# Last layer of a fused attention and MoE kernel: low parts one product later, weight work moved to other slots

## Chip, cores and metric

The kernel runs on one core of a Trainium2 chip. The metric is the device time of one execution in microseconds (us). A core has five engines that run beside each other, each with a queue of its own that it works through in order: TensorE (PE, with its weight loads as PEld), VectorE (DVE), ScalarE (ACT), GpSimd (POOL) and SyncE (SP, which here issues DMAs).

## What is computed

Attention with a window of 128 keys and four sink keys for every query, then a layer with eight experts, then a layer that multiplies two products elementwise:

```python
x = attention(q, k, v)                     # 1536 tokens x 512
P = sinkhorn(exp(x @ w_gate))              # 8 rounds, 1536 x 8
for e in range(8):                         # w1[e] 512 x 1024, w2[e] 1024 x 512
    out += P[:, e:e+1] * (np.maximum(x @ w1[e], 0) @ w2[e])
x = out
return ((x @ w_a) * (x @ w_b)) @ w_out     # w_a, w_b 512 x 1536, w_out 1536 x 512
```

All values are float32. The chip's fast matmul type drops bits, so a value is kept as a high part (a rounded copy) and a low part (value minus high part), and a product takes three matmuls: high x high, high x low, low x high (`mm3`, line 90).

## The kernel before

After the attention part, the two layers run as a row of steps. Tokens come in two batches of 768. The expert layer has 64 steps (`STEPS`): steps 0 to 31 are batch 0, 32 to 63 are batch 1. Each step takes one block of 256 hidden columns of one expert. The first matrix product of a step is done with a seven-product scheme (Strassen-like sums of blocks of x and of the weights): `product(s, j)` for j = 0 to 6, each six matmuls of 384 columns into a PSUM bank (128x384 in the profile). `leave(s, j, give)` takes the result out of the bank: j = 0 is an ACT copy (L353), 2 is the DVE sum at L357, 3 is L359, 4 the pair L369 and L370 (L364 and L365 in most steps of the expert layer), 5 is L373, 6 is L377 (L361 there). The last layer uses banks 6 and 7 in turn, so a product waits for the sum that empties its bank: product 4 for L357, product 5 for L359, product 0 of the next step for L373.

The last layer has twelve rounds q (`STEPS2`, six for each batch). A round is two steps, numbered on from 64: part 0 (x by `w_a`) and part 1 (x by `w_b`). In part 0, `keep` copies four results to `av[f][t]` (ACT, L567; f is the block of hidden columns, t the half of the batch). In part 1, `multiply` (L569 to L573) multiplies the kept value by the new one (DVE, L571), copies the high part to `hid` (ACT, L572) and hands the low part (`lower`, DVE, L169) to a list. It does so at product 1 for (f, t) = (0, 0), at product 4 for (1, 1), at product 5 for (0, 1); (1, 0) belongs to product 6 and is given one product later, in the next part 0.

Two lists set the order by hand. What is in `later` is issued at the end of the same product (`flush`), and what is in `late` moves to `later` then, so it is issued at the end of the product after it. The names `av` have tiles of their own: `first_p`, `room`, `room`, `extra`.

The second matrix product of round q - 1 runs in round q, six blocks of 128 tokens (`second2`, six matmuls of 512 columns each; 128x512 in the profile). In part 0 it does tokens 3, 4, 5 (half t = 1), in part 1 tokens 0, 1, 2. Its first block comes right after product 0 of part 0, and the third matmul of that block is the first that reads the low part (0, 1) of the round before. In rounds 1 to 4 (`turning`), batch 1 of x is transposed on TensorE beside this, and the blocks come after products 0, 1 and 5; in the other rounds after 0, 2 and 5.

Weights are prepared beside the matmuls. `pair_parts` makes one step's seven weight blocks: sums on POOL (L188, L191, L196, L204), high parts on ACT (L189, L193, L201, L208, L212, L218), low parts on DVE and, for the rows of the second product, on POOL (all L169: `ring<-raw` for loaded blocks, `ring<-room` for sums). `double_parts` packs a block of the last layer's weights to 29 bits a value and writes it back to memory (ACT L232, DVE L234, L235, L239, L243). A call of `work()` goes on with both by a bit. `quiet` (line 122) lists the expert steps at whose place in the queue of items one block is packed; there are 36. In the last layer `work()` is called once after every product, but not after product 0 of part 0 while x is turned.

In steps 31 and 32 the sums of x for the next batch are split too (`renew`, `flat<-xt` in the profile), on DVE for their low parts.

Of the kernel before, what the change touches and what calls it, by code (L numbers as in the profile page):

```python
# [33 lines left out]
PAIRS = NF // 2  # L34
# [12 lines left out]
def fused_kernel(  # L47
# [16 lines left out]
    pe, act, dve, pool, sp = nc.tensor, nc.scalar, nc.vector, nc.gpsimd, nc.sync  # L64
# [38 lines left out]
    STEPS, STEPS2 = B * E * PAIRS, B * PAIRS2  # L103
# [15 lines left out]

    quiet = [s for s in range(4, STEPS - 2) if s % PAIRS != 2 and abs(s - STEPS // 2 - 2) > 1]
    made = 0
    for s in range(STEPS):
        e, i = divmod(s % (E * PAIRS), PAIRS)
# [17 lines left out]
    def place(s):  # L143
        return s - 2 * (s >= STEPS + 2 * PAIRS2)
    loaded, taken, started, pairs = [0], [0], [0], [0]
    going, gone, ready, held = [], set(), set(), [False]
    later, late, whole = [], [], []
# [20 lines left out]
    def lower(src, hi, lo, eng):  # L168
        eng.tensor_tensor(out=lo, in0=src, in1=hi.bitcast(F32), op=ALU.subtract)  # L169
# [111 lines left out]
    def x_sums(x, space):  # L281

        t1, t2, t3, t4 = (space[:, n * S:(n + 1) * S].rearrange("p (k t) -> p k t", k=2) for n in range(4))
        b11, b12, b21, b22 = (x[:, 2 * i:2 * i + 2, j * HT:(j + 1) * HT] for i in range(2) for j in range(2))
        todo = [(t1, b12, b11), (t2, b22, t1), (t3, b22, b12), (t4, t2, b21)]
        return todo, [b11, b21, t2, t3, t1, b22, t4]
# [40 lines left out]
    def product(s, j):  # L327
        made_so_far[0] += 1
        ps = target(s, j)
        w = cell(CELLS * place(s) + ORDER[j])  # L330
        for kk in range(2):
            c0, c1 = slice(kk * 128, kk * 128 + 128), slice(256 + kk * 128, 384 + kk * 128)
            t0 = slice(kk * HT, kk * HT + HT)
            mm3(
                ps, w[:, c0], w[:, c1], x_part(j, 0)[:, t0], x_part(j, 1)[:, t0],
                kk == 0 and j != 1, kk == 1, check=j > 1,
            )
# [9 lines left out]
    def leave(s, j, give):  # L347

        ps = target(s, j)
        m = mid[:, s % 2 * 3:s % 2 * 3 + 3]  # L350
        m0 = m[:, 0] if s else first_p
        if j == 0:
            act.copy(out=m0, in_=ps)  # L353
        elif j == 1:
            give(s, ps, 0, 0)
        elif j == 2:
            dve.tensor_tensor(out=m0, in0=m0, in1=ps, op=ALU.add)  # L357
        elif j == 3:
            dve.tensor_tensor(out=m[:, 1], in0=m0, in1=ps, op=ALU.add)  # L359
        elif s in LONG and j == 6:  # L360
            dve.tensor_tensor(out=m[:, 2], in0=m[:, 1], in1=ps, op=ALU.subtract)  # L361
            give(s, m[:, 2], 1, 0)
        elif s in LONG and j == 4:
            dve.tensor_tensor(out=m[:, 1], in0=m[:, 1], in1=ps, op=ALU.add)  # L364
            dve.tensor_tensor(out=m0, in0=m0, in1=ps, op=ALU.add)  # L365
            give(s, m[:, 1], 1, 1)
            give(s, m0, 0, 1)
        elif j == 4:
            dve.tensor_tensor(out=m[:, 2], in0=m[:, 1], in1=ps, op=ALU.add)  # L369
            dve.tensor_tensor(out=m0, in0=m0, in1=ps, op=ALU.add)  # L370
            give(s, m[:, 2], 1, 1)
        elif j == 5:
            dve.tensor_tensor(out=m0, in0=m0, in1=ps, op=ALU.add)  # L373
            if s not in LONG:
                give(s, m0, 0, 1)
        else:
            dve.tensor_tensor(out=m[:, 1], in0=m[:, 1], in1=ps, op=ALU.subtract)  # L377
            late.append(lambda: give(s, m[:, 1], 1, 0))

    def flush():  # L380
        todo, later[:], late[:] = list(later), list(late), []
        for f in todo:
            f()
# [65 lines left out]
    def rest():  # L449
# [32 lines left out]
        def x2_turn(c, n, home):  # L482

            kk, half = divmod(n, 2)
            ps = home[:, 0:HT]
            for t in range(CB // 2):
                pe.transpose(  # L487
                    out=ps[:, t * 128:(t + 1) * 128],
                    in_=acc[c][:, half * (CB // 2) + t, kk * 128:(kk + 1) * 128], identity=ident,
                )  # L490
            act.copy(out=x2t[c][:, kk, half * HT:(half + 1) * HT], in_=ps)
# [6 lines left out]
        def halves(todo):  # L498

            return [tuple(t[:, k] for t in todo[n]) for n, k in ((0, 0), (0, 1), (2, 0), (1, 0), (3, 0), (2, 1), (1, 1), (3, 1))]  # L500
# [12 lines left out]
        def renew(plan, r, off=()):  # L513
            for n in plan[r] if r < len(plan) else ():
                later.append(x_split(ops, RANK[n // 2] if plan is EVEN else n // 2, pool if n in off else dve, slice(n % 2, n % 2 + 1)))
# [11 lines left out]
        for s in range(1, STEPS):  # L527
            long = s in LONG
            for r in range(7):
                j = RANK[r] if long else r  # L530
# [38 lines left out]
        def multiply(s, src, f, t):  # L569
            a, h, t0 = av[f][t], hid[s // 2 % 2], slice(t * HT, t * HT + HT)  # L570
            dve.tensor_tensor(out=a, in0=a, in1=src, op=ALU.mult)  # L571
            act.copy(out=h[:, 0, f, t0], in_=a)  # L572
            later.append(lambda: lower(a, h[:, 0, f, t0], h[:, 1, f, t0], dve))  # L573

        def second2(q, t, fs=(0, 1)):
            c, u = divmod(q, PAIRS2)
            h = hid[(STEPS // 2 + q) % 2]
            t0 = slice(t * 128, t * 128 + 128)
            last = u == PAIRS2 - 1 and fs != (1,)
            row = (c * CB + t) * 128  # L580
            for f in fs:
                n = CELLS * place(STEPS + 2 * q + 1) + 7 + 2 * f
                mm3(
                    bank[t], h[:, 0, f, t0], h[:, 1, f, t0], cell(n), cell(n + 1),
                    u == 0 and f == 0, last and f == fs[-1],
                )
            if not last:
                return

            end = q == STEPS2 - 1 and t == TURN[-1]  # L590
            for d in (slice(0, DM // 2), slice(DM // 2, DM)) if end else (slice(0, DM),):
                (dve.tensor_copy if d.start else act.copy)(out=acc[1][:, t, d], in_=bank[t][:, d])
                (act if d.start else sp).dma_start(out=out[row:row + 128, d], in_=acc[1][:, t, d])

        SUMS = ((3, 3), (3, 5), (4, 2), (4, 3), (4, 4), (5, 1), (5, 2), (5, 3))
        for q in range(STEPS2 + 1):
            c, u = divmod(q, PAIRS2)
            turning = 1 <= q < 5
            AT = (0, 1, 5) if turning else (0, 2, 5)
            for part in range(2):  # L600
                n = STEPS + 2 * q + part
                for j in range(7):
                    if q < STEPS2:
                        assert place(n) in ready, n
                        product(n, j)
                        leave(n, j, (keep, multiply)[part])
                    if turning and j == 1:
                        x2_turn(1, 2 * (q - 1) + part, bank[7])
                    if q == 0 and part == 0:
                        renew(FRONT, 7 + j, (12, 13))  # L610
                    if (q, part) in ((PAIRS2 - 1, 1), (PAIRS2, 0)):

                        held[0] = q == PAIRS2 and j < 5
                        renew(BACK, 7 * (q == PAIRS2) + j, (2, 3))
                    if j in AT:
                        t = TURN[3 * part + AT.index(j)]
                        if q == STEPS2 and part == 0:

                            if j == 0:
                                for x in TURN[0:3]:  # L620
                                    second2(q - 1, x, (1,))
                            second2(q - 1, t, (0,))
                        elif q:
                            second2(q - 1, t)
                        else:
                            second(STEPS - 1, t)
                    flush()
                    if (q, part, j) == (3, 0, 3):
                        todo, ops = x_sums(x2t[1], flat_0)
                        todo = halves(todo)  # L630
                    if part == 0 and (q, j) in SUMS:
                        step_sum(pool)
                    if not (turning and part == 0 and j == 0):
                        work()
                if q < STEPS2 and q != PAIRS2 - 1:
                    for m in range(7 if part else CELLS):
                        used[CELLS * place(n) + m] = True
            if q != PAIRS2:
                done = STEPS - 1 if q == 0 else place(STEPS + 2 * q - 1)
                for m in range(7, CELLS):  # L640
                    used[CELLS * done + m] = True
# [543 lines left out]
```

## Time and profile before

| | |
|---|---|
| median of 3 runs | 1391.4 us (1391.33 to 1391.56) |
| the profiled execution | 1391.5 us |
| its span, first to last instruction | 1389.7 us |
| PE busy | 1378.1 us, 99% of the span |
| DVE, ACT, POOL busy | 965.0, 578.8, 602.8 us |
| mean granted TensorE clock | 0.999 of 2.4 GHz |

The time of an execution is 1.8 us more than the span. TensorE is busy nearly always, but the ends of matmuls are modelled in this profile, so a short stop shows better as idle time of the weight loads (PEld), which run beside the matmuls. Expert step 32 begins at 587 us of the span, the last layer at 1090 us, its last matmul ends at 1384 us.

### The profile page before, as it was taken

How to read it: one execution, taken by the hardware profiler on the slowest of the kernel's cores; microseconds unless marked ns; L12 is line 12 of the kernel's file. 1: busy time of each engine (PE TensorE's matmuls, PEld its weight loads, DVE VectorE, ACT ScalarE, POOL GpSimd, SP SyncE). 2: the span in 40 equal slices, each digit the busy share in tenths (PEclk: the TensorE clock that was granted, in tenths of full speed). 3: DMA queues.
4: the chain of work that ended last, by engine and by line, in shares of the span. 5: the costliest groups of instructions: out<-in, count | busy, mean ns of one | idle time of the engine just before them, and what ended most of it. 6: DMA issues, size and time to landing. Idle time of an engine off the chain costs nothing.

```text
span 1389.7 us, 20344 instructions
## 1 busy us (share of the span) xinstructions
PE 1378.1 (99%) x7202; PEld 1222.8 (88%) x7202; DVE 965.0 (69%) x1886; ACT 578.8 (42%) x1322; POOL 602.8 (43%) x666
## 2 busy tenths in 40 slices
PE   9999999999999999999999999999999999999998
PEld 6678989898999999898899898989899898988997
DVE  7877776777686767865666777774656866777673
ACT  8873443433333333444333333333333544444442
POOL 7884343444434343343443434343433534523430
PEclk9999999999999999999999999999999999999999
DMA  7412332334333433323342333322222122213111
GB/s 228 127 47 84 114 106 92 106 100 123 100 111 94 119 106 92 106 69 99 97 123 85 110 106 103 114 89 74 66 68 69 54 69 61 77 38 99 61 32 48
DMA packets 144811, 127.37 MB, mean 92 GB/s; under 512 B 7844, under 2 KB 116004, under 8 KB 144700
## 3 DMA queue, kind: packets, MB, share of 16 engines
q1 hardware_dynamic: 144122, 125.46, 29.8%
q8 instruction: 58, 0.95, 0.3%
q10 hardware_dynamic: 578, 0.52, 0.1%
q14 instruction: 53, 0.43, 0.1%
HBM read 112.75 MB, written 12.58 MB: 90 GB/s over the span
## 4 chain that ended last, share of the span: by engine, by line
PE 94%; DVE 2%; ACT 1%; issue 1%; POOL 1%; DMA 0%; SPq 0%; DVEq 0%; ACTq 0%; POOLq 0%
PE bank L90 89%; PE bank L918 1%; PE bank L841 1%; PE bank L899 1%; PE bank L900 1%; POOL a L874 0%; PE bank L487 0%; DVE ring L169 0%; DVE hid L169 0%; ACT ex L858 0%; ACT hid L572 0%; PE bank L308 0%; PE bank L927 0%; DMA xt<-in_v 0%; DVE mid L373 0%
## 5 line engine op out<-in xcount | busy, mean ns | idle before, releaser
L90 PE MATMUL bank<-flat,ring 128*128 128x384 f32 x3696 | 688.5, 337 | 2.8 <-DVE mid L357 1.7
L90 PEld LDWEIGHTS bank<-flat,ring 128*128 128x128 f32 x3696 | 648.7, 188 | 28.8 <-DVE mid L357 4.2
L90 PE MATMUL bank<-ring,hid 128*128 128x512 f32 x2736 | 667.4, 393 | 0.4 <-DVE hid L169 0.4
L90 PEld LDWEIGHTS bank<-ring,hid 128*128 128x128 f32 x2736 | 508.1, 188 | 100.3 <-DVE hid L169 3.5
L169 POOL TENSOR_TENSOR ring<-raw,ring 128x512 fp32r<-128x512 f32 x150 | 211.1, 1426 | 399.3 <-ACT ring L201 390.7
L341 ACT ACTIVATE hid<-mid 128x384 fp32r<-128x384 f32 x191 | 97.0, 526 | 406.7 <-DVE mid L361 273.8
L188 POOL TENSOR_TENSOR room<-raw 128x256 f32<-128x256 f32 x86 | 88.5, 1029 | 298.6 <-DVE ring L169 109.0
L361 DVE TENSOR_TENSOR mid<-mid,bank 128x384 f32<-128x384 f32 x56 | 31.0, 554 | 132.4 <-PE bank L90 132.4
L169 DVE TENSOR_TENSOR ring<-raw,ring 128x512 fp32r<-128x512 f32 (+1 forms) x172 | 118.4, 689 | 0.0
L357 DVE TENSOR_TENSOR mid<-mid,bank 128x384 f32<-128x384 f32 x87 | 47.8, 550 | 98.9 <-PE bank L90 98.9
L169 DVE TENSOR_TENSOR ring<-room,ring 128x512 fp32r<-128x512 f32 x172 | 113.1, 692 | 2.8 <-ACT ring L212 2.8
L342 DVE SCALAR_TENSOR_TENSOR hid<-mid,hid 128x384 fp32r<-128x384 f32 x191 | 102.7, 562 | 13.0 <-ACT hid L341 4.9
L341 ACT ACTIVATE hid<-bank 128x384 fp32r<-128x384 f32 x64 | 31.5, 492 | 188.9 <-PE bank L90 188.7
L191 POOL TENSOR_TENSOR room<-raw 128x256 f32<-128x256 f32 x86 | 86.1, 1001 | 8.9 <-DVE ring L169 7.2
L204 POOL TENSOR_TENSOR room<-raw,room 128x256 f32<-128x256 f32 x86 | 71.6, 833 | 6.3
L373 DVE TENSOR_TENSOR mid<-mid,bank 128x384 f32<-128x384 f32 x87 | 48.0, 551 | 30.6 <-PE bank L90 30.5
L196 POOL TENSOR_TENSOR room<-room,raw 128x256 f32<-128x256 f32 x86 | 67.2, 782 | 0.0
L359 DVE TENSOR_TENSOR mid<-mid,bank 128x384 f32<-128x384 f32 x87 | 47.5, 545 | 11.0 <-PE bank L90 11.0
L218 ACT CAST ring<-room 128x512 fp32r<-128x512 f32 x86 | 52.9, 615 | 2.0 <-POOL room L204 1.7
L212 ACT CAST ring<-room 128x512 fp32r<-128x512 f32 x86 | 53.3, 620 | 0.9 <-POOL room L196 0.9
L239 DVE SCALAR_TENSOR_TENSOR room<-raw,room 128x512 int32<-128x512 int32 x36 | 52.8, 1468 | 1.1
L189 ACT CAST ring<-raw 128x512 fp32r<-128x512 f32 x86 | 53.5, 622 | 0.0
(150 smaller groups left out, 1152.7 us busy)
## 6 DMA issues: line engine op xcount, KB each, us to landing
raw<-in_moe_w SPq DMA_DIRECT2D x256, 256.0 KB, 2.6
raw<-kept SPq DMA_DIRECT2D x66, 256.0 KB, 3.1
kept<-room SPq DMA_DIRECT2D x36, 256.0 KB, 4.4
raw<-in_moe_w_a SPq DMA_DIRECT2D x12, 512.0 KB, 4.3
raw<-in_moe_w_b SPq DMA_DIRECT2D x12, 512.0 KB, 4.0
raw<-in_moe_w_out SPq DMA_DIRECT2D x12, 512.0 KB, 4.1
out_x<-xt SPq DMA_DIRECT2D x11, 256.0 KB, 2.0
qt<-in_q SPq DMA_DIRECT2D x6, 384.0 KB, 3.9
```

Source lines behind the costliest of these rows:

```text
L90: pe.matmul(out=dst, lhsT=a, rhs=b, start=start and n == 0, stop=stop and n == 2, skip_group_check=not check,)
L169: eng.tensor_tensor(out=lo, in0=src, in1=hi.bitcast(F32), op=ALU.subtract)
L188: pool.tensor_tensor(out=s1, in0=a21, in1=a22, op=ALU.add)
L189: act.copy(out=quads(hi, 4, 6), in_=firsts)
L191: pool.tensor_tensor(out=s3, in0=a11, in1=a21, op=ALU.subtract)
L196: pool.tensor_tensor(out=s2, in0=s1, in1=a11, op=ALU.subtract)
L204: pool.tensor_tensor(out=s4, in0=a12, in1=s2, op=ALU.subtract)
L212: act.copy(out=halves[0][0], in_=halves[0][2])
L218: act.copy(out=halves[1][0], in_=halves[1][2])
L239: dve.scalar_tensor_tensor(out=fi, in0=w[:, 0::2], scalar=29, in1=fi, op0=ALU.logical_shift_right, op1=ALU.bitwise_or)
L341: act.activation(out=h[:, 0, f, t0], in_=src, func=ACTF.Relu)
L342: later.append(lambda: dve.scalar_tensor_tensor(out=h[:, 1, f, t0], in0=src, scalar=0.0, in1=h[:, 0, f, t0].bitcast(F32), op0=ALU.max, op1 ...
```

## The change

There are three edits. `quiet` leaves out step 32 as well as 33 to 35 (34 was never in it), so the packing that stood at 32 and all those after it move on by one place in the list. `multiply` hands the low part to `late` in place of `later`, except for (1, 0) and in the last part of all. And in part 0 of the turning rounds the call of `work()` after product 2 is left out, and there are two after product 5.

```diff
-    quiet = [s for s in range(4, STEPS - 2) if s % PAIRS != 2 and abs(s - STEPS // 2 - 2) > 1]
+    quiet = [s for s in range(4, STEPS - 2) if s % PAIRS != 2 and not 0 <= s - STEPS // 2 < 4]
...
             a, h, t0 = av[f][t], hid[s // 2 % 2], slice(t * HT, t * HT + HT)
             dve.tensor_tensor(out=a, in0=a, in1=src, op=ALU.mult)
             act.copy(out=h[:, 0, f, t0], in_=a)
-            later.append(lambda: lower(a, h[:, 0, f, t0], h[:, 1, f, t0], dve))
+            soon = later if f > t or s == STEPS + 2 * STEPS2 - 1 else late
+            soon.append(lambda: lower(a, h[:, 0, f, t0], h[:, 1, f, t0], dve))
...
+        PACE = (1, 1, 1, 1, 1, 1, 1), (0, 1, 0, 1, 1, 2, 1)
...
-                    if not (turning and part == 0 and j == 0):
+                    for _ in range(PACE[turning and part == 0][j]):
                         work()
```

The order of TensorE's instructions stays as it was. Three places of DVE's queue change. In the rows below names carry numbers of buffers, which have no meaning here (`bank_69` and `bank_70` are banks 6 and 7).

First place: DVE in expert step 31, from the last low part of a weight block to the high-low split of the hidden block. Before:

```order
L169 TENSOR_TENSOR ring_1350<-raw_77,ring_1350 128x256
L234 TENSOR_SCALAR room<-room 128x512
L235 TENSOR_SCALAR room<-room 128x512
L239 SCALAR_TENSOR_TENSOR room<-raw_76,room 128x512
L357 TENSOR_TENSOR mid<-mid,bank_70 128x384
L169 TENSOR_TENSOR flat<-xt,flat 128x384
L243 SCALAR_TENSOR_TENSOR room<-raw_76,room 128x512
L342 SCALAR_TENSOR_TENSOR hid_1351<-bank_69,hid_1351 128x384
```

After:

```order
L169 TENSOR_TENSOR ring_1350<-raw_77,ring_1350 128x256
L357 TENSOR_TENSOR mid<-mid,bank_70 128x384
L169 TENSOR_TENSOR flat<-xt,flat 128x384
L342 SCALAR_TENSOR_TENSOR hid_1351<-bank_69,hid_1351 128x384
```

The four operations of one packing are gone from this step; the same four stand in step 54 now, in the same places round L357. No other step of the expert layer has another order on DVE.

Second place: DVE in part 1 of a turning round (step 67), from the sum of the part before to the sum of product 3. Before:

```order
L377 TENSOR_TENSOR mid<-mid,bank_70 128x384
L571 TENSOR_TENSOR first_p<-first_p,bank_69 128x384
L169 TENSOR_TENSOR hid_1351<-first_p,hid_1351 128x384
L169 TENSOR_TENSOR ring_75<-raw_76,ring_75 128x2x256
L357 TENSOR_TENSOR mid<-mid,bank_70 128x384
L169 TENSOR_TENSOR ring_75<-raw_76,ring_75 128x256
L359 TENSOR_TENSOR mid<-mid,bank_69 128x384
```

After:

```order
L377 TENSOR_TENSOR mid<-mid,bank_70 128x384
L571 TENSOR_TENSOR first_p<-first_p,bank_69 128x384
L169 TENSOR_TENSOR ring_75<-raw_76,ring_75 128x2x256
L357 TENSOR_TENSOR mid<-mid,bank_70 128x384
L169 TENSOR_TENSOR hid_1351<-first_p,hid_1351 128x384
L169 TENSOR_TENSOR ring_75<-raw_76,ring_75 128x256
L359 TENSOR_TENSOR mid<-mid,bank_69 128x384
```

The low part (0, 0), `hid<-first_p`, went from ahead of L357 to behind it, so that two low parts now stand between L357 and L359.

Third place: DVE from product 4 of step 67 over the end of the round into step 68. Before:

```order
L369 TENSOR_TENSOR mid<-mid,bank_70 128x384
L370 TENSOR_TENSOR mid<-mid,bank_70 128x384
L571 TENSOR_TENSOR extra<-extra,mid 128x384
L169 TENSOR_TENSOR hid_1351<-extra,hid_1351 128x384
L373 TENSOR_TENSOR mid<-mid,bank_69 128x384
L571 TENSOR_TENSOR room<-room,mid 128x384
L169 TENSOR_TENSOR hid_1351<-room,hid_1351 128x384
L169 TENSOR_TENSOR ring_75<-room,ring_75 128x2x256 x2
L377 TENSOR_TENSOR mid<-mid,bank_70 128x384
L571 TENSOR_TENSOR room<-room,mid 128x384
L169 TENSOR_TENSOR hid_1351<-room,hid_1351 128x384
L357 TENSOR_TENSOR mid<-mid,bank_70 128x384
```

After:

```order
L369 TENSOR_TENSOR mid<-mid,bank_70 128x384
L370 TENSOR_TENSOR mid<-mid,bank_70 128x384
L571 TENSOR_TENSOR extra<-extra,mid 128x384
L373 TENSOR_TENSOR mid<-mid,bank_69 128x384
L571 TENSOR_TENSOR room<-room,mid 128x384
L169 TENSOR_TENSOR hid_1351<-extra,hid_1351 128x384
L169 TENSOR_TENSOR ring_75<-room,ring_75 128x2x256 x2
L377 TENSOR_TENSOR mid<-mid,bank_70 128x384
L169 TENSOR_TENSOR hid_1351<-room,hid_1351 128x384
L571 TENSOR_TENSOR room<-room,mid 128x384
L169 TENSOR_TENSOR hid_1351<-room,hid_1351 128x384
L357 TENSOR_TENSOR mid<-mid,bank_70 128x384
```

The low part (1, 1), `hid<-extra`, moved behind the multiply of product 5, and the low part (0, 1), the first `hid<-room`, behind the two low parts of weights and L377. In part 0 of the turning rounds no low part of weights stands between L357 and L359 any more; both stand behind.

## Rows read from the trace of the kernel before

**Rows 1.** The page: span, and TensorE's busy time

```profile
span 1389.7 us, 20344 instructions
PE 1378.1 (99%) x7202; PEld 1222.8 (88%) x7202; DVE 965.0 (69%) x1886; ACT 578.8 (42%) x1322; POOL 602.8 (43%) x666
```

**Rows 2.** Waits of the weight loads, 1085 to 1385 us: total, times, longest

```profile
PEld bank L90 <- DVE hid L169: 3.5, 10, 0.9
PEld bank L90 <- DVE mid L357: 1.9, 6, 0.8
PEld bank L90 <- DVE mid L359: 1.4, 3, 0.7
PEld bank L90 <- DVE mid L373: 1.0, 2, 0.6
```

**Rows 3.** Timeline, step 31: start, duration, [idle before <-releaser]

```profile
574.62 1.51 DVE L234 TENSOR_SCALAR room<-room 128x512 f32<-128x512 f32 x1
576.16 1.40 DVE L235 TENSOR_SCALAR room<-room 128x512 int32<-128x512 int32 x1
577.60 0.69 DVE L239 SCALAR_TENSOR_TENSOR room<-raw,room 128x512 int32<-128x512 int32 x1
578.21 0.55 DVE L357 TENSOR_TENSOR mid<-mid,bank 128x384 f32<-128x384 f32 x1
578.81 0.30 PEld L90 LDWEIGHTS bank<-flat,ring 128*128 128x128 f32 x2 [1.52 <-DVE mid L357]
```

**Rows 4.** Timeline, DVE in step 46, which has a packing too

```profile
815.22 0.55 DVE L357 TENSOR_TENSOR mid<-mid,bank 128x384 f32<-128x384 f32 x1 [1.29 <-PE bank L90]
```

**Rows 5.** Timeline, steps 67 and 68: end of round 1, begin of round 2

```profile
1132.18 1.29 POOL L169 TENSOR_TENSOR ring<-raw,ring 128x512 fp32r<-128x512 f32 x1 [3.23 <-ACT ring L201]
1133.43 1.47 POOL L169 TENSOR_TENSOR ring<-raw,ring 128x512 fp32r<-128x512 f32 x1
1132.68 0.55 DVE L357 TENSOR_TENSOR mid<-mid,bank 128x384 f32<-128x384 f32 x1 [0.59 <-PE bank L90]
1133.15 0.60 DVE L169 TENSOR_TENSOR ring<-raw,ring 128x256 fp32r<-128x256 f32 x1
1133.72 0.55 DVE L359 TENSOR_TENSOR mid<-mid,bank 128x384 f32<-128x384 f32 x1
1134.76 0.55 DVE L369 TENSOR_TENSOR mid<-mid,bank 128x384 f32<-128x384 f32 x1 [0.49 <-PE bank L90]
1135.23 0.55 DVE L370 TENSOR_TENSOR mid<-mid,bank 128x384 f32<-128x384 f32 x1
1136.82 0.56 DVE L169 TENSOR_TENSOR hid<-extra,hid 128x384 fp32r<-128x384 f32 x1 [0.58 <-ACT hid L572]
1139.02 0.56 DVE L169 TENSOR_TENSOR hid<-room,hid 128x384 fp32r<-128x384 f32 x1 [0.58 <-ACT hid L572]
1139.49 1.28 DVE L169 TENSOR_TENSOR ring<-room,ring 128x512 fp32r<-128x512 f32 x2
1139.63 0.77 PEld L90 LDWEIGHTS bank<-ring,hid 128*128 128x128 f32 x4 [0.30 <-DVE hid L169]
```

**Rows 6.** Timeline, DVE and POOL in step 82

```profile
1310.10 0.74 POOL L196 TENSOR_TENSOR room<-room,raw 128x256 f32<-128x256 f32 x1
1310.92 0.94 POOL L204 TENSOR_TENSOR room<-raw,room 128x256 f32<-128x256 f32 x1
1310.13 1.13 DVE L169 TENSOR_TENSOR hid<-room,hid 128x384 fp32r<-128x384 f32 x1 [0.58 <-ACT hid L572]
1311.18 1.23 DVE L169 TENSOR_TENSOR ring<-raw,ring 128x512 fp32r<-128x512 f32 x1
```

**Rows 7.** Timeline, weight loads in parts 0 of steps 70, 74 and 78

```profile
1171.12 1.01 PEld L90 LDWEIGHTS bank<-flat,ring 128*128 128x128 f32 x6 [0.71 <-DVE mid L359]
1218.07 1.97 PEld L90 LDWEIGHTS bank<-flat,ring 128*128 128x128 f32 x11 [0.47 <-DVE mid L357]
1266.33 2.06 PEld L90 LDWEIGHTS bank<-flat,ring 128*128 128x128 f32 x12 [0.17 <-DVE mid L357]
```

## Prediction

> **What bounds the kernel.** I began with the page: TensorE is busy for 1378.1 of 1389.7 us [rows 1], so a change that leaves its instructions alone can only move its stops. The ends of matmuls are modelled, so I read the stops from the waits of the weight loads. In the last layer DVE causes nearly all: 3.5 us in ten waits for a low part of `hid`, 1.9 us for L357, 1.4 us for L359, 1.0 us for L373 [rows 2]. Outside it, one stop of 1.52 us stands in step 31 [rows 3]. These 9.3 us are all that the three edits can win. Two loads follow each other after some 0.05 us anyway, so a stop costs about 0.05 us less than its row says.
>
> Then I read the timeline at the end of a round, since all ten waits for `hid` are there, at the ends of rounds 1 to 10. The low part (0, 1) runs on DVE from 1139.02 for 0.56 us, so until 1139.58 [rows 5], and the weight load that needs it starts at 1139.63, idle before it for 0.30 us. So TensorE has no slack at this place: its position is set once a round by the end of that low part. What DVE does between TensorE's release of L369 and this end decides the round.
>
> **Step 31, the packing that moves.** L234, L235 and L239 take 1.51, 1.40 and 0.69 us ahead of L357, and TensorE waits for L357 for 1.52 us [rows 3]. Without them L357 can start when its product ends. I take a gain of 1.47 us. The four operations come back in step 54. In step 46, which has the same order of operations there, L357 still waited 1.29 us for TensorE [rows 4]: that is the cover, and I cost the move at nothing; if the cover failed as in step 31, it would cost 1.5 us. The place of the later packings and their loads moves by one item in the same pattern of steps, which I cost at nothing for the same reason.
>
> **Parts 0 of the last layer.** With no weight work between L357 and L359 in turning rounds, and with DVE earlier after the border of the round, these stops should go [rows 7]: 0.66 us in step 70, 0.42 us in step 74, and 0.12 us each in steps 78, 80, 82 and 84 (one of four equal rows stands there). That is 1.56 us. The call of `work()` that is moved past three products ends its weight block later, but the block is for a later step, and DVE waits for TensorE at L377 after it; cost nothing.
>
> **The end of a round.** Before, from the start of L369 to the end of the low part (0, 1), DVE needs 1139.58 - 1134.76 = 4.82 us, with two waits of 0.58 us for ACT's high parts [rows 5]. The change removes both waits, but puts more operations ahead of that low part: now L369, L370, multiply, L373, multiply, low part (1, 1), two low parts of weights, L377 and only then (0, 1). By the same rows, operations that depend on nothing follow after 0.47 us (L369 to L370), one that needs the result before it after 0.59 us, a low part of weights takes 0.60 us. So: three times 0.47, then 0.59 for L373, 0.47 for the multiply, 0.47 for (1, 1), 0.60 and 0.60 for the weights with 0.11 us of waiting for ACT's second sum copy, 0.47 for L377, 0.56 for the low part, and 0.09 more because POOL's next sum then runs: 5.37 us. The low part ends 0.55 us later, and with it TensorE's anchor. The ends of rounds 6 to 10 are like this (the last part keeps its order): 5 x 0.55 = +2.75 us. The bounds are +0.35 us (no wait for ACT or POOL) and +1.0 us (POOL's next sum goes first too). Round 5 has splits of x instead of weight blocks and stops there for 0.87 us already; I take no change, with bounds of -0.8 and +0.2.
>
> **The turning rounds.** In part 1 two low parts of DVE now stand between L357 and L359, while POOL makes its own two. What happens when both engines run such operations is seen in step 82 [rows 6]: a DVE low part that takes 0.56 us alone takes 1.13 us behind L196 of POOL, as if it began when L196 was through. The next POOL operation, L204, starts 0.08 us after L196 by its row, ends late, and the next DVE operation behind it takes 1.23 us where 0.69 us is usual [rows 5 and 6]. So the engines take turns. In step 67 [rows 5] POOL's first low part starts at 1132.18 for 1.29 us, its second at 1133.43; L357 starts at 1132.68. Now (0, 0) is next on DVE, at 1133.15, waits for POOL's first (free at about 1133.34) and ends at 1133.89. POOL's second then gets its turn. It ended 1.15 us after DVE's operation before (1134.90 against 1133.75), so now at 1135.04. The weight block's low part, 0.41 us alone, ends at 1135.31, and L359 runs from 1135.23 to 1135.78, where it began at 1133.72 before. L369 follows at 1135.70 in place of 1134.76, which is 0.94 us late, and the 5.37 us follow: the low part (0, 1) ends at 1141.07 instead of 1139.58, +1.49 us. In between product 5 stops for L359; that is inside this sum, since the anchor is what counts. Rounds 1 to 4 have the same rows: 4 x 1.49 = +5.96 us.
>
> *A rule beside this.* The turns are read from starts and ends of POOL's rows [rows 5 and 6]. The Trainium skill, in "Perfetto Trace Analysis", section "GPSIMD Engine Instruction", says that a GpSimd instruction's span in a profile is to be treated as unreliable. By the rows the turning rounds cost 5.96 us; by that page the order of starts would be open, and with it the first rival below.
>
> **Round 0.** Step 65 has the same operations between L357 and L359, and one more DVE sum among them. I take the same +1.49 us. Its bounds are +0.4 us (DVE goes first) and +2.7 us (the sum delays it further).
>
> **The sum.** -1.47 - 1.56 + 2.75 + 5.96 + 1.49 = +7.2 us. The durations are from the profiled execution, 1391.5 us (a span of 1389.7 and 1.8 around it), which makes 1398.7 us; the median of the runs is 0.1 us lower, so I predict 1398.6 us.
>
> **Rivals.**
>
> *DVE goes first.* If DVE's weight block gets in ahead of POOL's second low part in step 67, L359 ends at about 1134.7 and L369 is on time. Then the turning rounds cost 4 x 0.55 and round 0 some 0.9: -1.47 - 1.56 + 2.75 + 2.20 + 0.9 = +2.8, so 1394.2 us. Against it: the operation of POOL that was waiting went first [rows 6]. For it: the legend of the profile itself calls POOL's spans rough, and 0.4 us lie between the two starts in question (1133.43 and some 1133.8).
>
> *The waits go for good: faster.* If the low part (0, 1) ended before its load is due, which is 0.30 us before 1139.63 [rows 5], all the stops for DVE could go [rows 2, 3]: 9.3 us less some 20 times 0.05, 1383 us. It decides at one point: the chain from L369 must take under 4.5 us. The removal of two waits of 0.58 us speaks for it. Against it, nine operations of 0.47 to 0.60 us now stand ahead of this low part, and their busy time alone is over 4.5 us.
>
> *Little comes of it.* If the stalls at the ends of rounds turn out half as large, because weight blocks are done earlier than I think or stops merge, gains and losses cancel: 1391.4 us. That the change would not do what it says is ruled out by the order of DVE's queue; only its effect is open.
>
> **Chances and range.** A difference of over 0.2%, 2.8 us, is about what a measurement of this kernel can tell from no change. I give my forecast 0.64, DVE first 0.18 (half of it within 2.8 us, half above), little 0.09, the waits going for good 0.08, and 0.01 to more than 1401 us, where low parts lose their turn to POOL at every end of a round. So slower is 0.64 + 0.09 + 0.01 = 0.74, same 0.09 + 0.09 = 0.18, faster 0.08. The range takes in the forecast and DVE first, with their bounds: down to 1392.8 us (that rival with round 0 at +0.4 and all nine ends of rounds at +0.45) and up to 1400.8 us (the forecast with round 0 at +2.7 and rounds 6 to 10 at +0.75). The forecast alone reaches from 1396.5 us (round 0 at +0.4, rounds 6 to 10 at +0.35) to 1400.8 us.
>
> **What would show it.** In the changed profile step 31 has no stop for L357, and step 54 none. The load after the low part (0, 1) still waits for `hid`, 0.8 us in place of 0.30. In the turning parts 1 the weight loads wait about 1.4 us for L359, and DVE's weight low part ahead of it takes some 1.5 us. I am wrong if the round's end shows no wait for `hid`, or if L359 in step 67 comes within 0.5 us of L357's end.

## The result and the profile after

The changed kernel takes 1401.63 us (median of 6 runs, 1400.15 to 1403.4) where the kernel before takes 1391.37 us beside it (1391.21 to 1391.58): ratio 1.0073, interval 1.0063 to 1.0083. It is slower, as forecast, but the median lies 0.8 us above the forecast range. The profiled execution took 1400.16 us, with a span of 1398.4 us: 8.7 us more than the span before, where the sum said 7.2. Line numbers of the changed kernel are one higher from L573 on and two higher from L596 on; of the lines named here this concerns one alone, the output copy, which was L592 and is L593.

The page shows the same work as before [rows 1]:

```profile
span 1398.4 us, 20359 instructions
PE 1377.7 (99%) x7202; PEld 1224.3 (88%) x7202; DVE 964.2 (69%) x1886; ACT 580.2 (41%) x1322; POOL 607.5 (43%) x666
```

So the time went into stops. The waits of the weight loads in the last layer (total, times, longest), which answer to [rows 2]:

```profile
PEld bank L90 <- DVE hid L169: 10.4, 11, 2.3
PEld bank L90 <- DVE mid L359: 8.9, 6, 2.5
PEld bank L90 <- ACT acc L491: 1.1, 4, 0.3
PEld bank L90 <- DVE mid L373: 0.4, 1, 0.4
```

L357 is gone from the list, and the waits for L491 are as before (1.1 us in four). The waits for `hid` have tripled, those for L359 are six times as long. The stop in step 31 [rows 3] is gone too; DVE waits there for TensorE now:

```profile
576.58 0.55 DVE L357 TENSOR_TENSOR mid<-mid,bank 128x384 f32<-128x384 f32 x1 [2.48 <-PE bank L90]
```

In step 54, where the packing went, L357 keeps a margin of 1.29 us for TensorE, as the cover in [rows 4] said.

The timeline of DVE and POOL from the middle of step 67 to the load after the low part (0, 1), which answers to [rows 5]:

```profile
1132.95 2.85 POOL L169 TENSOR_TENSOR ring<-raw,ring 128x512 fp32r<-128x512 f32 x2 [2.24 <-ACT ring L201]
...
1133.45 0.55 DVE L357 TENSOR_TENSOR mid<-mid,bank 128x384 f32<-128x384 f32 x1 [1.73 <-PE bank L90]
1133.92 0.73 DVE L169 TENSOR_TENSOR hid<-first_p,hid 128x384 fp32r<-128x384 f32 x1
1134.58 1.50 DVE L169 TENSOR_TENSOR ring<-raw,ring 128x256 fp32r<-128x256 f32 x1
1136.00 0.54 DVE L359 TENSOR_TENSOR mid<-mid,bank 128x384 f32<-128x384 f32 x1
1136.65 0.55 DVE L369 TENSOR_TENSOR mid<-mid,bank 128x384 f32<-128x384 f32 x1
...
1136.60 1.00 PEld L90 LDWEIGHTS bank<-flat,ring 128*128 128x128 f32 x6 [1.42 <-DVE mid L359]
...
1141.37 0.63 DVE L169 TENSOR_TENSOR hid<-room,hid 128x384 fp32r<-128x384 f32 x1
...
1142.05 0.76 PEld L90 LDWEIGHTS bank<-ring,hid 128*128 128x128 f32 x4 [0.63 <-DVE hid L169]
```

From L357 to the end of the weight block's low part DVE needs 2.63 us here, and needed 1.07 us before. The low part (0, 1) then ends at 1142.00, 5.35 us after the start of L369; the sum said 5.37.

Round 0 is worse. In step 65 DVE and POOL do this:

```profile
1106.61 2.83 POOL L169 TENSOR_TENSOR ring<-raw,ring 128x512 fp32r<-128x512 f32 x2
...
1105.98 0.75 DVE L473 SCALAR_TENSOR_TENSOR xt<-bank,P,xt 128x512 f32<-128x512 f32 x1 [0.29 <-PE bank L90]
1106.65 1.67 DVE L169 TENSOR_TENSOR hid<-first_p,hid 128x384 fp32r<-128x384 f32 x1
1108.24 1.48 DVE L169 TENSOR_TENSOR ring<-raw,ring 128x256 fp32r<-128x256 f32 x1
1109.64 0.54 DVE L359 TENSOR_TENSOR mid<-mid,bank 128x384 f32<-128x384 f32 x1
...
1110.23 0.99 PEld L90 LDWEIGHTS bank<-flat,ring 128*128 128x128 f32 x6 [2.52 <-DVE mid L359]
```

Here POOL's first low part starts 0.04 us ahead of the low part (0, 0), which takes 1.67 us in place of 0.55, and the weight block's takes 1.48 in place of 0.42: both lose a turn. In step 67 POOL's first had started 0.97 us ahead of (0, 0) and was nearly through, so only the second of DVE's loses a turn in full.

The shift of the changed kernel against the one before, place by place, is read from the starts of the same matmuls in both traces (product 1 of a part 0 to the next; a stop of before that went is counted apart):

| place | forecast, us | measured, us |
|---|---|---|
| steps 31 and 35, stops for L357 gone | -1.47 | -1.80 |
| parts 0: steps 70, 74, and 78 to 84 | -1.56 | -1.64 |
| round 0 | +1.49 | +2.56 |
| rounds 1 to 4 | +5.96 | +6.50 |
| round 6 | +0.55 | +1.40 |
| rounds 7 to 10 | +2.20 | +1.84 |
| after the last round | 0 | -0.24 |
| sum | +7.2 | +8.6 |

Round 5, for which the forecast took no change, has no row of its own: its whole shift of -0.49 us stands in the second row. The stop of step 74 that went is most of it (0.42 us). Beside that, a stop for L359 in part 1 grew by 0.47 us and the stops at the end of the round shrank by 0.45 us, so that the forecast of no change came out by cancelling.

The table is for the profiled execution. That the median is 1.5 us above it is a second difference, and it lies in the spread of the runs. Before, 6 runs lie within 0.4 us; the changed kernel's 6 runs spread over 3.3 us, and their order is that of their mean granted clock: 0.999 in those of 1400.15 and 1400.16 us, 0.998 in those of 1401.32, 1401.94 and 1402.16 us, 0.997 in that of 1403.4 us.

### The profile page after: what moved, and what is told of

Its sections match the earlier page's. It is cut to its first block, busy times and chain, and to the rows that moved or that the text cites. A ratio compares the mean times of both kernels' runs of the same rounds, so it can differ in the third digit from the quotient of the medians.

```text
span 1398.4 us, 20359 instructions
## 1 busy us (share of the span) xinstructions
PE 1377.7 (99%) x7202; PEld 1224.3 (88%) x7202; DVE 964.2 (69%) x1886; ACT 580.2 (41%) x1322; POOL 607.5 (43%) x666
## 4 chain that ended last, share of the span: by engine, by line
PE 92%; DVE 4%; ACT 2%; issue 1%; POOL 0%; DVEq 0%; ACTq 0%
PE bank L90 86%; PE bank L920 1%; PE bank L843 1%; DVE ring L169 1%; ACT hid L572 1%; PE bank L901 1%; DVE hid L169 1%; PE bank L902 1%; DVE mid L369 0%; ACT ex L860 0%; ACT ring L218 0%; PE bank L487 0%; DVE mid L377 0%; DVE mid L370 0%; DVE extra L571 0%
## 5 line engine op out<-in xcount | busy, mean ns | idle before, releaser
L357 DVE TENSOR_TENSOR mid<-mid,bank 128x384 f32<-128x384 f32 x87 | 47.9, 550 | 112.8 <-PE bank L90 112.5
L359 DVE TENSOR_TENSOR mid<-mid,bank 128x384 f32<-128x384 f32 x87 | 47.6, 547 | 25.2 <-PE bank L90 25.2
L353 ACT COPY mid<-bank 128x384 f32<-128x384 f32 x87 | 40.7, 468 | 40.8 <-PE bank L90 40.8
L218 ACT CAST ring<-room 128x512 fp32r<-128x512 f32 x86 | 52.8, 614 | 1.5 <-POOL room L204 1.5
```

The lines of the kernel that those rows point to most:

```text
L218: act.copy(out=halves[1][0], in_=halves[1][2])
```

## The experiments

Theory, once the two traces had been laid side by side: the time comes from two places, the turns of DVE and POOL in parts 1 of rounds 0 to 4, and the low part (0, 1) standing behind the weight block at every end of a round. The main rival: a kernel with more operations between L357 and L359 is slower whatever POOL does. The runs of before beside each experiment lie between 1391.3 and 1391.6 us in their medians.

**The same kernel again**, to find where the spread arises.

> The changed kernel itself, again. Its six runs spread over 3.2 us, those of before over 0.4 us, and the profiled one was among the fastest. Theory A (DVE and POOL race at the ends of rounds): in the profile of the change the second low part of weights starts 40 ns ahead of POOL's next sum (L188) at the ends of rounds 1 to 4 and 7 to 9; where POOL comes first, the low part (0, 1) is some 0.6 us later. Then the runs spread over 1400 to 1404 us again, and a profile that is over 1401 us shows one or more ends of rounds with a low part of weights of 1 us or more behind L188. Theory B (the spread comes from elsewhere, loads or the attention part): a profile that is slower has its extra time before 1090 us.

1401.43 us (1400.32 to 1403.36). Both theories missed. The shifts of rounds 1 to 10 repeat to 0.03 us, and those of the expert layer to 0.15 us. Only round 0 differs: +3.84 us in place of +2.56. The windows round its stop, first of this run, then of the first profile of the changed kernel (busy time and count of PE, PEld, DVE, ACT and POOL, granted clock, DMA):

```profile
1105.00:1110.00 5.00, 2.86 (x16) 2.41 (x14) 4.71 (x6) 1.05 (x3) 4.18 (x4) 1.00 0.17 52
1110.00:1111.00 1.00, 0.95 (x5) 0.95 (x6) 0.90 (x2) 0.00 (x0) 0.00 (x0) 1.00 0.00 0
1111.00:1114.00 3.00, 3.00 (x10) 2.42 (x9) 1.67 (x4) 2.06 (x4) 0.00 (x0) 0.51 0.85 256
```

```profile
1111.00:1114.00 3.00, 3.00 (x17) 2.73 (x16) 2.80 (x6) 2.07 (x4) 0.00 (x0) 1.00 0.75 256
```

After the stop of 2.5 us for L359 the granted clock is 0.51 here, which is the level of 1.2 GHz, and TensorE gets through 10 matmuls in place of 17. The stop itself is as long in both. So the spread lies in the clock, which falls behind a long stop in some executions and not in others.

**One edit at a time.** First the packing alone:

```diff
-    quiet = [s for s in range(4, STEPS - 2) if s % PAIRS != 2 and abs(s - STEPS // 2 - 2) > 1]
+    quiet = [s for s in range(4, STEPS - 2) if s % PAIRS != 2 and not 0 <= s - STEPS // 2 < 4]
```

> Only the list of quiet steps is changed; the last layer is as before. My working: the stop of step 31 goes (1.5 us), as it did in the changed kernel, and the one of 0.3 us in step 35 too; 1389.6 us, step 54 without a stop. Rival: the packing only moves the stop to step 54; 1391.4 us.

1389.5 us (1389.01 to 1389.92), ratio 0.9987, interval 0.9978 to 0.9996: a gain of 1.8 us, of which 1.47 lie in step 31, and 0.29 in step 35, where a stop of 0.34 us for L357 goes that the forecast had not looked for.

Then the calls of `work()` alone:

```diff
+        PACE = (1, 1, 1, 1, 1, 1, 1), (0, 1, 0, 1, 1, 2, 1)
...
-                    if not (turning and part == 0 and j == 0):
+                    for _ in range(PACE[turning and part == 0][j]):
```

> Only the calls of work() in part 0 of the turning rounds are moved; low parts and quiet steps are as before. My working: the stop of 0.7 us in step 70 goes and nothing else moves: 1390.7 us. Rival: the two calls after product 5 put weight blocks ahead of L377 and cost at the next part: 1391.5 to 1393 us.

1390.76 us (1390.34 to 1391.28), ratio 0.9996, interval 0.9986 to 1.0005: within what can be told from no change, and in the trace the stop of step 70 alone is gone.

And the low parts alone (the list `late`, with `quiet` and `work()` as before):

> Only the low parts go one product later; quiet steps and calls of work() are as before. If the whole loss comes from the low parts, this is slower than the changed kernel by what the other two edits gain there, 1.8 us and about 0.7 us: 1402.5 to 1404.5 us. Rival: the moved calls of work() take part in the loss (two low parts of weights at the end of part 0); then this is no slower than the changed kernel: 1399 to 1402 us.

1405.51 us (1402.9 to 1406.22), ratio 1.0097, interval 1.0082 to 1.0112. The loss is all in this edit. It came out above the expectation, and the profile says why: the granted clock falls three times in it, once early on in the attention part, at 10.8 us of the span (+0.9 us by step 31), once after the stop of round 0 and once after that of round 6.

**Which low part.** Of the late edit, one of the three alone, with the other two edits undone:

```diff
-            soon = later if f > t or s == STEPS + 2 * STEPS2 - 1 else late
+            soon = late if (f, t) in ((0, 0),) and s < STEPS + 2 * STEPS2 - 1 else later
```

> Only the low part of product 1 goes one product later, the other two at once; all else as before. My theory (turns between DVE and POOL): two low parts of DVE stand between L357 and L359 while POOL makes two, L369 comes 0.94 us late in each of the four turning rounds and later still in round 0, where the changed kernel stopped 2.4 us for L359: 3.8 + 1 to 2.5 us, 1396 to 1398 us, with weight loads that wait over 1 us for L359 in steps 65, 67, 69, 71, 73. Rival (the loss is at the ends of rounds alone, where a low part is queued behind weights): this one costs nothing, 1390.5 to 1391.5 us.

1398.67 us (1397.33 to 1399.9), ratio 1.0051, interval 1.0035 to 1.0066: a bit above the expected 1396 to 1398. The turning rounds take 1.15 us more each, round 0 2.8 us with a fall of the clock in it, round 5 0.3 us, and rounds 6 to 10 nothing.

With `(0, 1)` in its place, product 5's:

> Only the low part of product 5 goes one product later; all else as before. My theory: it is the one that TensorE awaits at the end of the round, and it now stands behind two low parts of weights and L377. From L369: 0.94 us to the multiply, its low part at once until 2.64, L373, the multiply, two low parts of weights that wait for ACT until 5.5, L377, the low part until 6.4 to 6.6 us where it was 4.82: 1.6 to 1.8 us in each of ten rounds, 1407 to 1409 us, more if TensorE's clock falls after such stops. Rival (turns between DVE and POOL at L359 make the loss): 1391.4 us, or up to 1393.

1418.53 us (1417.48 to 1419.81), ratio 1.0198, interval 1.0182 to 1.0213. A clear miss on the far side: the waits for `hid` are 24.6 us in 11 stops (longest 2.7), and the clock falls five times. Rounds 1 and 2, where it does not fall, cost 2.0 us each, where 1.6 to 1.8 had been expected. The step by which it is worse than the whole change is read from DVE at the end of round 1:

```profile
1138.64 0.56 DVE L169 TENSOR_TENSOR hid<-extra,hid 128x384 fp32r<-128x384 f32 x1 [0.58 <-ACT hid L572]
...
1141.36 0.87 DVE L169 TENSOR_TENSOR ring<-room,ring 128x512 fp32r<-128x512 f32 x1 [0.50 <-ACT ring L218]
1142.15 0.54 DVE L377 TENSOR_TENSOR mid<-mid,bank 128x384 f32<-128x384 f32 x1
1142.62 0.83 DVE L169 TENSOR_TENSOR hid<-room,hid 128x384 fp32r<-128x384 f32 x1
...
1143.50 0.53 PEld L90 LDWEIGHTS bank<-ring,hid 128*128 128x128 f32 x3 [2.34 <-DVE hid L169]
```

It has the weight block ahead of the low part (0, 1), as in the change, and keeps the wait of 0.58 us for ACT at (1, 1), which the change removes; the second weight low part then waits 0.50 us more for ACT's L218. So the three parts do not add up: alone they cost +1.15, +2.0 and -0.24 us in such a round, together 1.63.

With `(1, 1)`, product 4's:

> Only the low part of product 4 goes one product later; all else as before. It then stands behind the multiply of product 5 and right ahead of the low part of product 5, with no weights between. My theory: both waits of DVE for ACT shrink, the awaited low part ends 3.7 us after L369 begins where it was 4.82, before its load is due; the ten waits at the ends of rounds go (0.17 us of TensorE each, 0.9 us in round 5) and the stop of 0.5 us for L373 in step 77: 1388 to 1389 us. Rival (any low part that is put off costs): above 1391.4 us.

1387.59 us (1387.44 to 1388.02), ratio 0.9973, interval 0.9963 to 0.9983: faster than before by 3.9 us, and 0.4 us below the expected range. At the end of round 1 DVE now runs without a wait for ACT:

```profile
1136.69 0.56 DVE L571 TENSOR_TENSOR room<-room,mid 128x384 f32<-128x384 f32 x1
1137.16 0.55 DVE L169 TENSOR_TENSOR hid<-extra,hid 128x384 fp32r<-128x384 f32 x1
1137.83 0.56 DVE L169 TENSOR_TENSOR hid<-room,hid 128x384 fp32r<-128x384 f32 x1
1138.30 1.28 DVE L169 TENSOR_TENSOR ring<-room,ring 128x512 fp32r<-128x512 f32 x2
...
1138.85 1.28 PEld L90 LDWEIGHTS bank<-ring,hid 128*128 128x128 f32 x6
```

The low part (1, 1) fills the time in which ACT makes the high part of (0, 1), the two waits of 0.58 us [rows 5] have become one gap of 0.12 us, and the load has no stop. No wait for `hid` is left in the last layer. The stops of steps 70 and 74 and those of steps 78 to 84 [rows 7] are gone too, which the expectation did not count. A new stop of 0.77 us for L359 stands in part 0 of round 4, step 72.

**Is it POOL?** The changed kernel without POOL's own low parts of weights in parts 1 of rounds 0 to 4:

```diff
-            lower(v[:, 0], cells[:, 7], cells[:, 8], pool)
+            now[0] in MUTE or lower(v[:, 0], cells[:, 7], cells[:, 8], pool)
...
-            lower(v[:, 1], cells[:, 9], cells[:, 10], pool)
+            now[0] in MUTE or lower(v[:, 1], cells[:, 9], cells[:, 10], pool)
```

(`now[0]` is the step, `MUTE` is 65, 67, 69, 71, 73.)

> The changed kernel, but POOL's ten low parts of weights in steps 65, 67, 69, 71 and 73 are left out (the low parts of these rows of w_out keep old values), nothing else moves on any queue. Theory A (DVE and POOL take turns, so a weight low part of DVE that comes behind the low part (0, 0) waits for POOL's second one): the four stops of 1.26 us for L359 in steps 67 to 73 and the stop of 2.4 us in step 65 go, DVE's 128x256 low part takes 0.4 us in place of 1.5, the shift of a turning round falls from 1.63 to 0.5 us (0.3 to 0.7) and that of round 0 from 2.6 to 0.5 us (0 to 0.7), the waits for hid at the ends of these rounds stay: profiled run 1400.2 - 4 x 1.1 - 2.1 = 1393.7 us (1392.8 to 1394.8). Theory B (one more operation between L357 and L359 is enough, POOL has no part in it): the stops for L359 stay over 1 us, 1399 to 1402 us.

1395.1 us (1393.0 to 1395.5). DVE in step 67, against the rows above:

```profile
1131.30 0.56 DVE L357 TENSOR_TENSOR mid<-mid,bank 128x384 f32<-128x384 f32 x1 [1.72 <-PE bank L90]
1131.77 0.55 DVE L169 TENSOR_TENSOR hid<-first_p,hid 128x384 fp32r<-128x384 f32 x1
1132.23 0.42 DVE L169 TENSOR_TENSOR ring<-raw,ring 128x256 fp32r<-128x256 f32 x1
1132.57 0.55 DVE L359 TENSOR_TENSOR mid<-mid,bank 128x384 f32<-128x384 f32 x1
```

The same four operations in the same order, and 1.50 us have become 0.42. The shift of a turning round falls from 1.63 to 0.50 us, that of round 0 from 2.56 to 0.37 us. So the rival is out: with one more operation there, two stops of 0.15 us are all that is left of the stops for L359 in rounds 1 to 4, while POOL's turns cost 1.1 us a round. The median is above the expected range; in the profiled run the granted clock falls after the stop of 2.3 us at the end of round 6 (rounds 6 and 7 shift by 3.3 us together there, in place of 1.8), and the shortest run, 1393.0 us at a mean clock of 1.0, is inside the range.

**Is it the clock?** The changed kernel with the low parts of steps 65 and 77 alone as before, so that no stop of 2 us or more is left:

```diff
-            soon = later if f > t or s == STEPS + 2 * STEPS2 - 1 else late
+            soon = later if f > t or s in (65, 77, 87) else late
```

> The changed kernel, with the low parts of steps 65 and 77 alone handed out as before, so that the two stops of over 2 us (round 0, and the end of round 6) are gone and all stops of up to 1.3 us stay. Theory A (TensorE's granted clock falls in some executions after these two stops, and that makes the spread of 3 us and the 1.3 us by which the median is over the profiled run): 1400.2 - 2.6 - 1.4 = 1396.2 us for the profiled run, granted clock at 1.0 throughout the steps, median within 0.4 us of the profiled run, all runs within 1 us. Theory B (the spread comes from the turning rounds' stops of 1.3 us): the runs still spread over 2 to 3 us, median 1397 to 1398 us.

1396.47 us (1396.29 to 1396.6), ratio 1.0037, interval 1.0023 to 1.0051. The spread of 3 us is gone with the two stops, the median is 0.2 us from the profiled run, and the four waits of 1.4 us for L359 in the turning rounds are still there. Theory A holds.

**Why round 6 is worse than rounds 7 to 10.** At its end ACT copies an output block of batch 0 (L593). In the profile of the changed kernel:

```profile
1265.02 0.58 ACT L593 COPY xt<-bank 128x512 f32<-128x512 f32 x1
1265.50 0.62 ACT L218 CAST ring<-room 128x512 fp32r<-128x512 f32 x1
...
1266.15 0.86 DVE L169 TENSOR_TENSOR ring<-room,ring 128x512 fp32r<-128x512 f32 x1 [0.51 <-ACT ring L218]
1266.93 0.54 DVE L377 TENSOR_TENSOR mid<-mid,bank 128x384 f32<-128x384 f32 x1
1267.40 0.83 DVE L169 TENSOR_TENSOR hid<-room,hid 128x384 fp32r<-128x384 f32 x1
...
1268.28 0.76 PEld L90 LDWEIGHTS bank<-ring,hid 128*128 128x128 f32 x4 [2.33 <-DVE hid L169]
```

That copy was left out, and step 65 kept as before so that its clock does not disturb:

```diff
-                (dve.tensor_copy if d.start else act.copy)(out=acc[1][:, t, d], in_=bank[t][:, d])
+                (q, t) == (PAIRS2 - 1, TURN[5]) or (dve.tensor_copy if d.start else act.copy)(out=acc[1][:, t, d], in_=bank[t][:, d])
```

> The changed kernel with the low parts of step 65 handed out as before (so the long stop of round 0 is gone), and without ACT's copy of the last output block of batch 0 at the end of round 6 (that block of the output keeps old values). Theory A (the output copy stands ahead of L218 on ACT, so the second weight low part and with it the low part (0, 1) come late): DVE no longer waits 0.51 us for L218 at the end of round 6, the wait for hid there falls from 2.3 to some 1.5 us or less, and rounds 6 and 7 together shift by 0.9 us in place of 1.8: 1400.2 - 2.6 - 0.9 = 1396.7 us, the runs within 1 us. Theory B (the end of round 6 is longer for another reason, POOL's next sums or the stop in step 76): the wait stays over 2 us, 1397.6 us for the profiled run and 1398 to 1400 us where the clock falls after it.

1397.13 us (1396.93 to 1397.27). The wait for `hid` at this place is 1.47 us in place of 2.33, and the shift of round 6 is +0.53 us in place of +1.40, which is the 0.55 of the forecast. By its time alone the run lies between the two theories; the place decides for A, with rounds 6 and 7 at 0.91 us together. Of the 0.5 us by which the profiled run (1397.23 us) is above the sum of A, 0.4 us lie behind the start of the last matmul (6.40 us to the end, 6.03 in the change). DVE and the load at this place:

```profile
1262.47 1.41 DVE L169 TENSOR_TENSOR ring<-room,ring 128x512 fp32r<-128x512 f32 x2
1263.80 0.55 DVE L377 TENSOR_TENSOR mid<-mid,bank 128x384 f32<-128x384 f32 x1
1264.26 0.62 DVE L169 TENSOR_TENSOR hid<-room,hid 128x384 fp32r<-128x384 f32 x1
...
1264.93 0.76 PEld L90 LDWEIGHTS bank<-ring,hid 128*128 128x128 f32 x4 [1.47 <-DVE hid L169]
```

**A version that beats both.** The change with `late` for (1, 1) alone, so with the packing and the calls of `work()` as changed:

```diff
-            soon = later if f > t or s == STEPS + 2 * STEPS2 - 1 else late
+            soon = late if (f, t) in ((1, 1),) and s < STEPS + 2 * STEPS2 - 1 else later
```

> Quiet steps and calls of work() as in the changed kernel, but of the low parts only that of product 4 is put off. If the three gains add: 1.8 us (quiet steps), 0.6 us (calls of work()), some 3 us (the low part): 1386 us. If the last two win the same stops: 1386.7 us.

1385.18 us (1385.09 to 1385.51), ratio 0.9955, interval 0.9942 to 0.9969: 6.3 us faster than before. The gains add up in their total: 3.9 of (1, 1), 1.8 of the packing, 0.6 of `work()`. That is in part luck. Two of the edits do win the same stop, that of step 70: it is all that the calls of `work()` remove alone, and it is gone with (1, 1) alone too. Together they remove the new stop of step 72 as well, and round 4 shifts by -0.23 us in place of +0.52.

And with the call of `work()` after product 1 of step 65 given after product 5, since the largest stops left stand there (0.64 us for L357, 0.31 us for L359, in matmul starts):

```diff
-        PACE = (1, 1, 1, 1, 1, 1, 1), (0, 1, 0, 1, 1, 2, 1)
+        PACE = (1, 1, 1, 1, 1, 1, 1), (0, 1, 0, 1, 1, 2, 1), (1, 0, 1, 1, 1, 2, 1)
...
-                    for _ in range(PACE[turning and part == 0][j]):
+                    for _ in range(PACE[2 if n == STEPS + 1 else turning and part == 0][j]):
```

> The best version so far (1385.2 us) with step 65's call of work after product 1 given after product 5, so that the weight block's 128x512 low part runs behind L357 and L473 on DVE, no longer ahead of L357, and the 128x256 one behind L359. The stop of 0.64 us for L357 in step 65 goes; of the 0.41 us for L359 some stays or it grows to 0.6, since the 128x512 low part now stands ahead of it. If POOL's low parts keep out of the way 1384.2 us, if the 128x512 one has to wait for a turn of POOL's 1385.2 us (nothing won). Expected 1384.5 us.

1384.96 us (1384.75 to 1385.27), ratio 0.9955, interval 0.9941 to 0.9968: no gain that can be told. The stop for L357 went, but the 128x512 low part moved in ahead of L359, took 1.35 us beside POOL's first low part, and the stop for L359 grew to 0.84 us.

## Why the prediction was wrong

**Right: the bound and the direction.** TensorE's position is set once a round by the low part (0, 1). The late edit removes both waits for ACT and puts the weight block and L377 ahead of that low part: 5.37 us were forecast from L369 to its end, 5.35 were measured. The load behind it was to wait 0.8 us for `hid` and waits 0.63. The gain in step 31 (-1.47, measured -1.47), the cover in step 54 and the stops of parts 0 (-1.56, measured -1.64) are as forecast. Round 5 at no change is right by luck, as said below the table.

**Right: the turns.** That L359 falls behind POOL in the turning rounds was forecast at +1.49 us a round and measured at +1.63; without POOL's low parts it is 0.50. The first rival (DVE goes first) was priced at 0.55 for such a round and fell. The Trainium skill, "Perfetto Trace Analysis", section "GPSIMD Engine Instruction", says to treat the span of a GpSimd instruction as unreliable and to time such instructions by the spacing of their starts; that the order of starts would be open is the prediction's own inference. Here the starts and ends of POOL's rows gave the order of the turns and the loss of a round to 0.14 us.

**Wrong: the term for round 0.** "I take the same +1.49 us", with a bound of +2.7. It measured +2.56. The step that failed is the assumption that step 65 has the rhythm of step 67. One DVE sum more (L473) stands ahead of the low part (0, 0), which so comes just behind the start of POOL's first, and both low parts lose a full turn: 1.12 and 1.06 us over their time alone, against 0.18 and 1.08 in step 67. That the turns make this loss is shown by the run without POOL's low parts, where round 0 shifts by 0.37 us; that L473 sets their order is read from the starts, and no run moved it.

**Wrong: the term for round 6.** "The ends of rounds 6 to 10 are like this." Round 6 has ACT's output copy ahead of L218, and cost 1.40 in place of 0.55; without the copy it costs 0.53. The rows for it were in the trace of before:

```profile
1259.58 0.51 ACT L572 CAST hid<-room 128x384 fp32r<-128x384 f32 x1 [1.15 <-DVE room L571]
1260.00 0.58 ACT L592 COPY xt<-bank 128x512 f32<-128x512 f32 x1
1260.47 0.62 ACT L218 CAST ring<-room 128x512 fp32r<-128x512 f32 x1
...
1260.60 1.29 DVE L169 TENSOR_TENSOR ring<-room,ring 128x512 fp32r<-128x512 f32 x2
```

L218 ended at 1261.09, 1.0 us after ACT's high part for the low part (0, 1). DVE came to the second low part of that weight block late enough not to wait, because of its own two waits for ACT; once these are gone it comes early, and waits 0.51 us for L218.

**Wrong: the clock was not in the sum.** This is the step that put the median outside the range. The prediction has no term for the granted clock and gives no reason for that; in the profile of before it was 1.0 all through the steps, where no stop exceeded 1.52 us. The change makes two stops of 2.3 to 2.5 us, and behind these the clock falls to 1.2 GHz in some executions, which costs 1.3 to 1.6 us each time (round 0: 3.84 against 2.56; round 7 of the low parts alone: 1.92 against 0.37). The profiled execution, without such a fall, is at 1400.16 us still inside the forecast range, with both wrong terms in it; the one of the second profile, with a fall in round 0, took 1401.43 us. Of the other executions only the mean clocks are known: 0.998 in the three round the median, 0.999 in the two fastest, which fits one fall more in each of the three. With the two long stops gone the spread went too.

**Small.** Step 35 gave 0.29 us that had not been looked for, and rounds 7 to 10 cost 0.46 us each in place of 0.55. The upper end of the range counts rounds 6 to 10 at +0.75 us, though the bound given for such an end is +1.0; with that bound it is 1402.0 us and takes in the median, but the clock is still not in it.

## What to carry to other kernels

An operation that is put off by one slot lands behind whatever that slot holds: read what is queued there on its engine, and who shares a resource with it, before calling the delay free. Of three operations put off together here one gained 0.2 to 0.3 us in most rounds and the other two lost far more, so an edit of this kind should be tried one operation at a time. And price a stop of TensorE by its length as well as by the sum: here stops of 1.4 us and less cost their length in every run, and two of over 2 us cost the clock as well in some, which shows as a spread of the runs.

## What the runs showed of the hardware

DVE and POOL take turns on operations whose operands all lie in SBUF, and a turn is a whole operation: a 128x256 low part that takes 0.42 us alone takes 1.48 to 1.50 us beside two of POOL's. An operation of DVE with an operand in PSUM did not wait: L359 takes 0.55 us beside POOL's second low part [rows 5], and L357 in step 67 of the change 0.55 us beside POOL's first. With this the Trainium skill agrees in "SBUF — State Buffer", section "SBUF: two separate sides", where DVE and GpSimd share a pair of ports by an exclusive lock that DVE needs for two inputs in SBUF, and that is held for the whole instruction.

TensorE's granted clock fell after stops of 2.3 and 2.5 us in some executions, and in others of the same kernel stayed at 1.0 after the same stop (0.51 and 1.00 in the two windows shown). In both TensorE had been at work up to the stop and went on at once behind it. In the run of (0, 1) alone five of seven stops of 2.3 us at the ends of rounds have a fall behind them; one of 2.65 us has none, and the three of 1.8 to 1.9 us have none. A stop of over 2 us is not needed everywhere: in the run of the low parts alone the clock fell in the attention part as well, at 10.8 us, where the waits of the weight loads just before it were 0.8 us at most. What decides was not found out.
